# A gated recurrence joined to a PReLU block on one core: level products taken in threes, three tiles folded into one, and a new written-out order

## The chip, the cores and the metric

The kernel runs on one core of a Trainium2 chip. The metric is device time in microseconds (us) for one launch. The engines that matter are TensorE (PE in the profile; its weight loads are PEld), VectorE (DVE), ScalarE (ACT), GpSimd (POOL) and SyncE (SP), which issues every DMA of this kernel.

## What is computed

A complex gated linear recurrence per batch and head, and then two matrix products with a PReLU between them:

```python
# B, H, S, D = 4, 8, 768, 48
a_n = (a_re, a_im) * min(mag, 0.999) / (mag + 1e-6)      # mag = |a|
for t in range(S):
    S_c = a_n[t][:, None] * S_c + outer(k[t], v[t])      # S_c complex, D x D per head
    y[t] = q[t] @ real(S_c)
x = y as (B*S, H*D)                                      # 3072 x 384
h = x @ w_in                                             # 384 x 2048
g = max(h, 0) + alpha * min(h, 0)
out = g @ w_out                                          # 2048 x 384
```

All of it is in fp32, and every product is an fp32 product on PE.

## The kernel before

The sequence is cut into chunks of 128 tokens. One chunk of one batch, with all 8 heads, is a unit; there are 4 x 6 = 24 units, and units 0 to 5 are the chunks of batch 0.

**Gates.** `gates` runs seven times (one, two and three chunks for batch 0, then three chunks each). It turns `a_re` and `a_im` into phases, which are running products of the unit-length gates, and into decays, which are products of the magnitudes over 1, 2, 4, ... tokens. Both go out to DRAM (`phs`, `decs`) and come back for each unit as the tiles `PP` (phases) and `T` (decays, 96 x 8 x 256). Most of the gates' instructions are DVE's (L257 to L425) and ACT's.

**A unit.** `unit` first turns queries and keys, both in the tile `KQ` (96 partitions: real and imaginary parts of 48 dimensions), by their phases: one DVE product over 2048 elements per partition (L648). The tokens of the chunk then interact in six levels, h = 1, 2, 4, 8, 16, 32. In level h, blocks of h tokens are taken in pairs, and the queries of the second block of a pair meet the keys of the first. The loop over levels does four things for each h:

- ACT copies the keys' half of that level into a packed tile `W` (L719, 512 elements; not for h = 1).
- `meet` issues 32 small products on PE into a PSUM tile `lv` (L662); the queries are read as strided halves of `KQ`. Each fp32 product stands in the trace as two matmuls, so a level shows as x32 with 16 products for each of two halves of the heads.
- `step` multiplies `KQ` in place by the decays of that level (L701, DVE, 1024 elements), which also makes it ready for the next level. Since it writes what `meet` reads, it waits for PE.
- `mask_out` moves `lv` to `A{h}` under a mask, on DVE (L686) for h up to 8 and on ACT (L683) for 16 and 32.

After the levels the keys are transposed on PE (L736) and copied by ACT into the tile `KT` (L738). PE multiplies them with `V` into the chunk's contribution to the state (L747), multiplies the `A` tiles with the values `VL` into `Y` (L768), and adds the part of the incoming state (L793). DVE moves the state on (L777, L780). ACT copies `Y` to the tile `yT` (L807), SP writes that to DRAM (`ysc`, L812) and reads it back as `xT` (L825).

**The matrix products.** `features` makes 128 rows of `h` with three matmuls (L841), ACT takes the negative part (L848), DVE adds the scaled rest (L850). `outputs` multiplies by `w_out` (L860), ACT moves the sums out (L870), SP writes them (L873). These products run for one or two units at a time, as soon as their `xT` is there.

**What sets the order.** Each of these parts is a Python generator that yields before each instruction. The string `ORDER` says which generator goes on next, letter by letter (A to G the gates, J to N the loads and weights, O to l the units, n and o the matrix products). It was written by a planner ahead of time; the costs in `yield DVE(...)`, the rings `R[...]` and the names in `done` are that planner's input and do nothing on the chip. Each engine therefore runs a fixed queue, in order, and waits on semaphores that the tile framework sets from the data. A tile that is allocated again waits until its last reader is through: `T` has two buffers, `KQ` three, `V` and `VL` one.

Of the kernel before, what the change touches and what calls it, by code (L numbers as in the profile page):

```python
# [18 lines left out]
P = 128  # L19
# [11 lines left out]
    "AAAAAAAAAABBAMMABMAAAAAMNAAAMMAAAAAAAAABKAAAAAAJKBBNBAKJANAAAJONNAAAAAAOBNOAAAAAAAAAAAJAAAKKAAAAAAKK"  # L31
    "KBABKLMAMKKKAAAAAAAAAAAAABBAAAAAAAAAALLLNLNOBBBBBBBBBBBBBBBOKKLJBBJBCOCNBBBBNNBBBNNNKNBBNNBBBBBOPBBO"
    "BBOOBBBBBBBLLBBBBBPCPPBBBBBBBBBBBOBJBBBBCBBBNBCBBJBPMMJBLBBBLBOPBLMLJJJPPBBCLBOBONOPBBMCCCCCPNPPCLCN"
    "CCCNNCCOPPKJCPCCJMPPJJJJPCNCOCCCCCCCCPOOOOCCCONNNPPQQCOCMCMDPPPPPPPPPPPPPPPPPNPPCNCNCCCNCPONPOCCCQCN"
    "NPKCQCCCPCPCJQQQPQQQCCCCOCCCCQCPNOJQQCOJDJPJJPPKQPDDONJDQCCCCCCCCCQCCOOCQCDQQOLOCCCCCCCDKMRnQQQMKQQK"
    "KKNCKOKOCCCCKMRJQoOCCQQQQNQoJCDQoCCOCLOCCNCCQONLoooLLLDLLDNNDLLDoooDDLoRoNLoRDoRNNDRDRooLLNRJRRDDDDD"
    "NQRoRQKoQQQRDKDJQEREoDONJDDDMDDDQooooDoDooooooRQooooooQooEDoooDoRRRRoooOooOOooooooDRRRJRoJDSooooooRD"
    "RoRRLooQQooELoSOOOLLLLLLLDDDLLLRQQQSRRKKoLDEooSoQooOoDRooRooLoSoDoooEDDooRoooRRROSRRRREoooooQRREDDDD"
    "SDDDDDDoDEESJJSJEEQDJJRJJJSKSSSTSDDLLLRRRRRRLLLESSSDLLTSDEnToTDDSTSETTSSSSLSJTSSSLLDDDDDDDDEEDDDDooS"
    "LLLoKTSooJSoEooSEoDDDDSEETSSSSSSJJSSSSETTTDJEEETDJooEEEEoUTJJJJLLoEooEEJTooDSoooooEoooTDDDTDoSSSSSoL"  # L40
    "LLLLLLooooUTooULLooEooooULJETDTooDooooooDDTDUoooTTooooLooDUoDooKLTTDooooTToooooDDDTETToUUoooTooToTTT"
    "TTnoDoooooooooTLLLUUoooKooLLLLLUTUoLooLooFEJLTUUUULoooooEoJUEooooooUUUUUUEJooEULEEooooooooUoTKEEEToo"
    "EEUVoTToTUUoEoooVVoooooEooooooVUJVVoUFoVUUooTVoUVVUVEUUJJJJUEEEEEEEEEEEEUoUJJTLTVUVFVoVoFWooFVJVVooo"
    "VFooooUUUVVVJUWVKVVUVWWoooooVLLWLLLLLWLLEEEEEEEEEEEEEEEELVVoVLLoWWoLJVVoWoVUoVWVVVooEooooJEEUWWWoVVV"
    "VWVVVVoWWJJJJJJXooEFnFooEEoEELLLLLLLLKJEFLoooVEoooEEooLEooWLLLWXoWLooooWWEoooEooooKEXEWWWKoVVooooooo"
    "KXooEooooXWJWJXXoooWooooWWFoVVoWVXWooooooWWFXFWWWFEWWFFFFGFXooLJLLLLLLXWooooooWFWFXXJFoooFooooFWoFXX"
    "oLLFoGooooJJooooooJFoWFXXXFWFFFWFFFoFooWFoXFFWXooooooFooooooooooXXXXYooooooooGJFWWFXXFXYooFFoooXLLXX"
    "LFFooooooooooLoooYXGLoooXJoooooGYXXFXXFFXXXXXFFFFFFFJYYFJnYJXoGYoooooJFFFFFFFFFFFFFFFLFJJYZFoooooooL"
    "ooGoYZYXXXGJYYZooXooZZoGoooooYooYXoFooooYYYYYYYYYZZoooZFZFFFooooFXJYZoLLLoYoYJYoLLLLLLLKYoYoYooZGLLY"
    "YKYYYYJFYZYYJKXFFFGGooYYJYLLLJLFFLoooooaFFFoYLFFFoFoJJJooZLFZYYYGYYaGLoLLoLLooooooooFLLFoFFFoooooooo"  # L50
    "ooooZoooaZaJZaoooGoZaJZnGZZZZZaooooooooooooaaooaGaZZoooaooZoJoooJGoZZooZoZoooZaHZZZGGoGGGGGGGZZZZZGZ"
    "GaZKKHLGGGoooooaGGoooooooGooobooGoaoooaoaaaaaoooLoGGbooobbZaaaoaaZooaJZZZLJoLLLLLLLLLLoGGGGaaoooGboG"
    "GJoooZaJJoabboooooooaaaaaaaaGHJZHGJJbbbbGGGLGGooooooHoooobaobJJaGGGGGGGGaaaooJJboocooooooobbcoGGbcHb"
    "ooGbLJJKooooooooooooocbGbHcHcLGLcGGKooooooLLbHbLcbbaabGGGGGGooooobbKcGbGJGJGcLLGGGooooHGGcobbbcHoooo"
    "bbLooooLLLLbbbnbcGHbbbbbJGGGdoooooGoLLoocbGGGGGccbooooJJboooGKobGGoGHooLLLLLLoooGHbbbboLooooooooGcLL"
    "LdddccccHdooooocccooooooocdcccdooJoddoLoooooHJcdocLHdJoHdHKHdcoJJooooooocccccIIccoccceooJJooHLLLoooo"
    "oooLoLdeLcHHcccHHHHccccoLLLHHLHHHHnooHoHHHLooooooooHJooooeIdLLLooooooooddooooooeeeHHHHdooHoHHdHeeooo"
    "oooooodddddeooooooodJdoJoeooHHHHHHHHHHHoodoodododeoododooodeedddddddHHdHHHHHHIeeKKeeKHJJooJfooooIooo"
    "ooeeeKeddfoLLdeeooeoeoooJooLooooddLLHHHHHHHHHHHHHHJeedIeeeLfooLLoLLooefLLLLeIofdooeeeHHeeeeeeHHefIIf"
    "IfHfJHHJHJdJooooooeeJJJJJeeeoeegLJHLHHLLofoLLLLLLLofIoooooooooIHooLJffooJoHoooooHogofHoHHIoooooIoooo"  # L60
    "noffoHHooooogfoofoooooffIffffLgoogoooofgooLoffIfJoofoIfIIooJoIfoofooooffffffffffgKggooooohLLLooLhogo"
    "oIoLgghgoooooJJILLLoooLLLffILLfhIIIgghoooooooooohgooJJhgfJJfhhKffggIgggKgooohoooohhggggJghooohoogogo"
    "IgIgooooggIgggggggIhJhoLLgLgIIIIJgIogooooKKoIoooIhooLooILhIoooooooggKJIIIIIIIIJJoooooiLIhoooIIIIoIoo"
    "oooihnooIhhhhihhiooooIiooooLLLLLLiihhLLohohoooooohohohoooohhIIIIhhIhhhhhhJJJIooooooooooJJLiioihiioio"
    "JIoLooLiiijoooooIIIooooIIIioIIIIIIIIIIoiiiiiihhhhhjLLhjLoLLLLLLLiJIIIIIIIoooooojooooojoiijjjoooiooio"
    "jiiooooiLhIIIIIoIoioiiiiiiJLLLLLILooooooLLoooiIioooiiiiiIijjoIiiiIIooooooooooooonJooJJJJooojjjjooooo"
    "ooooooooooooJoLLjjoojojjoojoLkojLjjoooooooooojjkokoooooojjkkjookkoooojjjooLooooLjkjjjjJkkooojjkjjkoo"
    "oooJoooooooookJJokjjJJLllLooLokLkoLoLLLjjkkLkkkLLLLLkkjJjjkooooooooooooJkollkokkJoooooooooookllllooj"
    "kokooJJJlJokoooookkkkJkkkkkkkkkllLLlkLLooomkkkoooolooooooLollooooolloJooomloooonoooooooooooooooooooo"
    "oooooooooollllJlmmooooooooooolmmlooooooolllooolLLLLolomLLLLLllooooooooollloolmlmmmmoooooooomlllloooo"  # L70
    "ooooooooooomlmlmlmoolommllllnoooooooooooooommLmmmoooooooooooooooooooooooooomoLomLooooomommoLLLLLoooL"
    "LLmmmLLooooooooooooooooooooooooooooooooooooooooooommmmmmmmmoommmmmoooooomnoooooooooooooooooooooooooo"
# [30 lines left out]
def kernel(  # L103
# [46 lines left out]
    LEVELS = [1 << i for i in range(6)]  # L150
# [16 lines left out]
    masks, by_row = {}, {}  # L167

    def mask(h):

        m = work.tile([P, P // h, h], F32, tag="W", name="mask", bufs=2)
# [12 lines left out]
    for h in (16, 32):  # L184
        by_row[h] = []
        for m in range(HC // h):
            t = consts.tile([P, 1], F32, tag=f"rows{h}_{m}", name=f"rows{h}_{m}")
            nc.vector.tensor_reduce(out=t, in_=ident.rearrange("p (i m h) -> p m i h", i=2, h=h)[:, m],
                                    axis=mybir.AxisListType.XY, op=ALU.add)
            by_row[h].append(t)  # L190
# [5 lines left out]
    def step(*args, **kwargs):  # L196
# [5 lines left out]
        KQ=3, PP=1, T=2, V=1, W=2, KT=1, St=3, yT=1, xT=2, raw0=1, raw1=1, raw2=1, g0=0, g1=0, g2=0, ot=2, top=2,  # L202
# [7 lines left out]
    bias_tiny = consts.tile([P, 1], F32, tag="bias_tiny")  # L210
    nc.vector.memset(bias_tiny, TINY)
    bias_one = consts.tile([P, 1], F32, tag="bias_one")
# [8 lines left out]
    def gates(g, b, c0, c1):  # L221
# [139 lines left out]
        def three(dst, re_im, k, t):  # L361

            yield ACT(1.5 * k, t)
            nc.scalar.copy(dst[:, 1:3], re_im)
            t = yield ACT(k, t)
            nc.scalar.activation(dst[:, 0], re_im[:, 1], AF.Copy, scale=-1.0)  # L366
            return t
# [585 lines left out]
```

## Time and profile before

| | us |
|---|---|
| median of 3 runs | 863.18 (861.69 to 864.44) |
| the profiled execution, its own time | 859.8 |
| its span on the core | 858.1 |
| PE busy | 704.7 |
| DVE busy | 655.6 |
| ACT busy | 427.1 |
| POOL busy | 186.3 |
| first of the `features` matmuls (L841) starts at | 129.9 |

The span is the time from the first to the last instruction; 1.7 us lie around it. A group's line gives source line, engine, operation, tiles and shapes, the count, the busy time, the mean duration of one, and then the engine's idle time just ahead of these instructions with what ended it. PE's matmuls overlap each other, so a matmul's duration is longer than its distance to the next one: in the rows of the timeline, work is read from start to start.

### The profile page before, as it was taken

What the parts mean: (1) busy time and instruction counts of PE and PEld (TensorE: products, weight loads), DVE (VectorE), ACT (ScalarE), POOL (GpSimd) and SP (SyncE); (2) the same over time, 40 slices, a digit from 0 to 9 for tenths busy, and PEclk for the clock granted to TensorE, in tenths of its full rate; (3) what the DMA queues carried; (4) which work ended last, traced back from release to release, by engine and by line L of the source; (5) the groups of instructions that cost most, each with busy time, mean ns of one, the idle gap of its engine ahead of it and who ended that gap; (6) DMA issues with size and microseconds to landing.
All of it is one profiled execution on the core that took longest, in us unless ns stands there. A gap on an engine that the chain in (4) does not pass through costs nothing.

```text
span 858.1 us, 26855 instructions
## 1 busy us (share of the span) xinstructions
PE 704.7 (82%) x11488; PEld 529.1 (62%) x11488; DVE 655.6 (76%) x996; ACT 427.1 (50%) x913; POOL 186.3 (22%) x293
## 2 busy tenths in 40 slices
PE   0000414976898999999999999999999999999998
PEld 0000313655676777777777777777777777777776
DVE  5999999999976899789978987798867665444212
ACT  7757578576434565554555554654334234233221
POOL 5212323457313200440034005300052000000000
PEclk9999965896999999999999999999999999999999
DMA  7689977977688778669684787865674766221110
GB/s 222 170 211 232 269 175 178 241 154 154 170 194 165 159 195 207 125 135 227 160 182 110 180 216 147 158 170 127 176 155 74 173 121 134 63 51 38 39 39 9
DMA packets 194559, 130.92 MB, mean 153 GB/s; under 512 B 74504, under 2 KB 186248, under 8 KB 194440
## 3 DMA queue, kind: packets, MB, share of 16 engines
q1 hardware_dynamic: 194440, 129.20, 64.9%
q8 instruction: 90, 1.47, 0.8%
q14 instruction: 29, 0.24, 0.1%
HBM read 100.82 MB, written 35.71 MB: 159 GB/s over the span
## 4 chain that ended last, share of the span: by engine, by line
PE 74%; DVE 15%; SPq 3%; issue 3%; DMA 3%; ACT 2%; DVEq 0%; ACTq 0%
PE ps_o L860 29%; PE ps_h L841 29%; PE ps_lv L662 5%; PE ps_y L768 4%; DVE KQ L701 3%; PE ps_kv L747 3%; PE ps_y L793 3%; SPq L556 2%; DVE gate L336 2%; PE ps_kt L736 2%; DMA V<-in_v_dram 1%; DVE gate L338 1%; DVE gate L316 1%; DVE gate L296 1%; DVE gate L422 1%
## 5 line engine op out<-in xcount | busy, mean ns | idle before, releaser
L841 PE MATMUL ps_h<-xT,w_in_sb 128*128 128x256 f32 (+1 forms) x1344 | 303.4, 357 | 0.0
L860 PE MATMUL ps_o<-w_out_sb,g_sb 128*128 128x384 f32 x768 | 297.5, 501 | 7.2 <-DVE g_sb L850 7.1
L841 PEld LDWEIGHTS ps_h<-xT,w_in_sb 128*128 128x128 f32 x1344 | 233.8, 193 | 69.9 <-issue 1.7
L701 DVE TENSOR_TENSOR KQ<-KQ,T 96x1024 f32<-96x1024 f32 x144 | 178.3, 1248 | 44.1 <-PE ps_lv L662 41.1
L848 ACT ACTIVATE g_sb<-ps_h 128x256 f32<-128x256 f32 (+1 forms) x224 | 78.9, 353 | 235.8 <-PE ps_h L841 235.1
L850 DVE SCALAR_TENSOR_TENSOR g_sb<-g_sb,al,ps_h 128x256 f32<-128x256 f32 (+1 forms) x224 | 97.5, 437 | 126.8 <-ACT g_sb L848 126.4
L860 PEld LDWEIGHTS ps_o<-w_out_sb,g_sb 128*128 128x128 f32 x768 | 137.4, 192 | 58.0 <-DVE g_sb L850 9.7
L662 PE MATMUL ps_lv<-KQ,W 96*32 96x32 f32 x3840 | 56.5, 205 | 57.5 <-ACT W L719 54.1
L719 ACT COPY W<-KQ 96x512 f32<-96x512 f32 x120 | 74.3, 623 | 55.4 <-DVE KQ L701 54.1
L662 PEld LDWEIGHTS ps_lv<-KQ,W 96*32 96x32 f32 x3840 | 44.6, 116 | 83.0 <-ACT W L719 62.4
L662 PE MATMUL ps_lv<-KQ 96*32 96x32 f32 x768 | 12.0, 206 | 68.2 <-DVE KQ L648 52.6
L511 POOL TENSOR_SCALAR top<-top 128x768 f32<-128x768 f32 x16 | 43.5, 2721 | 84.3 <-ACT top L503 84.0
L648 DVE TENSOR_TENSOR KQ<-KQ,PP 96x2048 f32<-96x2048 f32 x24 | 55.0, 2292 | 0.0
L662 PEld LDWEIGHTS ps_lv<-KQ 96*32 96x32 f32 x768 | 9.5, 119 | 71.8 <-DVE KQ L648 52.6
L336 DVE TENSOR_TENSOR gate<-gate 128x576 f32<-128x576 f32 (+5 forms) x84 | 48.3, 575 | 3.1 <-ACT gate L308 1.3
L768 PE MATMUL ps_y<-A,VL 64*48 64x64 f32 x2304 | 42.2, 223 | 8.6 <-issue 6.8
L683 ACT ACTIVATE A<-ps_lv,rows 128x64 f32<-128x64 f32 x144 | 39.2, 331 | 19.4 <-PE ps_lv L662 19.0
L336 POOL TENSOR_TENSOR gate<-gate 128x72 f32<-128x72 f32 x42 | 19.0, 451 | 127.2 <-ACT gate L366 124.4
L768 PEld LDWEIGHTS ps_y<-A,VL 64*48 64x48 f32 x2304 | 39.6, 125 | 11.0 <-issue 8.9
L422 DVE TENSOR_TENSOR gate<-gate 128x1152 f32<-128x1152 f32 (+2 forms) x36 | 43.5, 1233 | 0.1
L807 ACT COPY yT<-ps_y 48x256 f32<-48x256 f32 x96 | 32.0, 366 | 21.1 <-PE ps_y L793 20.4
L686 DVE TENSOR_TENSOR A<-ps_lv,mask 128x256 f32<-128x256 f32 x96 | 39.5, 414 | 0.0
(100 smaller groups left out, 774.5 us busy)
## 6 DMA issues: line engine op xcount, KB each, us to landing
T<-decs SPq DMA_DIRECT2D x48, 384.0 KB
PP<-phs SPq DMA_DIRECT2D x48, 193.5 KB
KQ<-in_q_dram SPq DMA_DIRECT2D x48, 192.0 KB
decs<-gate SPq DMA_DIRECT2D x7, 1152.0 KB
phs<-gate SPq DMA_DIRECT2D x14, 576.0 KB
KQ<-in_k_dram SPq DMA_DIRECT2D x40, 192.0 KB
vsc<-in_v_dram SPq DMA_DIRECT2D x48, 144.0 KB
VL<-vsc SPq DMA_DIRECT2D x24, 288.0 KB
```

The lines of the kernel that those rows point to most:

```text
L336: on(4 * k).tensor_tensor(out=m, in0=w[:, 1::-1].unsqueeze(2).to_broadcast([P, 2, 2, k]), in1=pairs_of(u), op=ALU.mult)
L422: TT(out=m[:, a], in0=U5[:, 1 + a], in1=turned(off3, o)[:, a].unsqueeze(1).unsqueeze(3).to_broadcast([P, L // 2, nb, 2]), op=ALU.mult)
L511: nc.gpsimd.tensor_scalar(out=top, in0=top, scalar1=F64_SMALL, scalar2=None, op0=ALU.max)
L648: nc.vector.tensor_tensor(out=KQ, in0=KQ, in1=bass.AP(tensor=PP.tensor, offset=PP.offset, ap=[PP.ap[0], (1, 2), (P + 1, H), (1, P)]), op=A ...
L662: nc.tensor.matmul(t[64 * i + j:64 * i + j + HC // 2, p], lhsT=weights(4 * i + p)[:, j:j + HC // 2], rhs=q_[:, m * g:m * (g + 1)], start=T ...
L701: nc.vector.tensor_tensor(out=x, in0=x, in1=m, op=ALU.mult)
L719: nc.scalar.copy(W.rearrange("p n t -> p (n t)").rearrange("p (m h) -> p m h", h=h), halves(KQ[:, 1].rearrange("p n t -> p (n t)"), h)[:, ...
L768: nc.tensor.matmul(o, lhsT=Vp[h][64 * i:64 * i + 64, s, e_ * D:(e_ + 1) * D], rhs=a, start=False, stop=False)
L841: nc.tensor.matmul(p, lhsT=w_in_sb[:, f // 2, kk, f % 2 * P:(f % 2 + 1) * P], rhs=x_of[m][:, kk], start=(kk == 0), stop=(kk == NK - 1))
L848: nc.scalar.activation(gt, p, AF.Relu, scale=-1.0)
L850: nc.vector.scalar_tensor_tensor(out=gt, in0=gt, scalar=al_1[:, f:f + 1], in1=p, op0=ALU.mult, op1=ALU.add)
L860: nc.tensor.matmul(sums[0], lhsT=gt[:, c * P:(c + 1) * P], rhs=w_out_sb[:, f], start=(f == 0), stop=(f == NF - 1))
```

## The change

- Levels are taken in two visits, (1, 2, 4) and (8, 16, 32). Within a visit the products of the three levels are issued one after the other on PE, into three parts of one `lv` tile; they wait until the last level's operands are there.
- For the first two levels of a visit, keys and queries come from a copy: for h = 1 it is written by the turn itself, whose one product over 2048 elements becomes two over 1024 (one into the copy `WQ`, one in place); for h = 2, 8 and 16 ACT copies both halves (1024 elements instead of 512). For h = 4 ACT copies the keys alone as before, for h = 32 nothing is copied. So `step` no longer waits for PE in four levels of six, but for ACT's copy in three of these.
- The three `mask_out` of a visit follow the last product.
- `KT` and `yT` are gone. The transposed keys go to the first 128 columns of the decays' tile `T` (in two ACT copies per half instead of one, since the padding is now filled from PSUM), and the outputs go to the same columns later. `T` is therefore free only when the unit's outputs have left for DRAM, and no longer after the state's update.
- Small constant tiles are put into one; `run`, `runs` and `begin` of the gates have one buffer instead of two; `mask` uses a `WQ` buffer.
- `ORDER` is written anew as a whole.

The numbers of products, DMAs and gate instructions stay as they were: PE has 2304 level products in the program before and after, SP 755 DMAs.

```diff
 ORDER = (
-    "AAAAAAAAAABBAMMABMAAAAAMNAAAMMAAAAAAAAABKAAAAAAJKBBNBAKJANAAAJONNAAAAAAOBNOAAAAAAAAAAAJAAAKKAAAAAAKK"
...
+    "AAAAAAAAAAAAAAAAAAMMMMBAANBJAAAAANMMNJJAAAAAAAAAAAONAAAANAAAOOAANAAAAAAAAAAAAAJANOAOBNAAAAMMKNLNAAAL"
...
-    LEVELS = [1 << i for i in range(6)]
+    VISITS = [(1, 2, 4), (8, 16, 32)]
+    LEVELS = [h for visit in VISITS for h in visit]
...
-                    L["T"] = T = work.tile([D2, H, TL], F32, tag="T", name="T", bufs=2)
+                    L["T"] = T = work.tile([P, H, TL], F32, tag="T", name="T", bufs=2)
...
-        nc.vector.tensor_tensor(out=KQ, in0=KQ, in1=bass.AP(
-            tensor=PP.tensor, offset=PP.offset, ap=[PP.ap[0], (1, 2), (P + 1, H), (1, P)]), op=ALU.mult)
...
+        WQ = work.tile([D2, 2, H, HC], F32, tag=f"WQ{first_slot}", name="WQ", bufs=1)
+        nc.vector.tensor_tensor(out=WQ, in0=some(1, -1), in1=phases(1, 0), op=ALU.mult)
+        r = yield DVE(H * P)
+        nc.vector.tensor_tensor(out=some(0, 1), in0=some(0, 1), in1=phases(0, 2), op=ALU.mult)
...
-            t = ps.tile([P, HP, HC // 2], F32, tag="lv", name="ps_lv", bufs=2)
+            if not shared:
+                shared.append(ps.tile([P, 3, HP, HC // 2], F32, tag="lv", name="ps_lv", bufs=2))
+            t = shared[0][:, at]
...
-        for h in LEVELS:
-            w = k_
-            if h == 1:
-                weights = lambda n: KQ[:, 1, n].rearrange("p (m s) -> p m s", s=2)[:, :, 0]
-            else:
-                w = yield ACT(H * HC, k_, takes=(R["W"],))
-                W = work.tile([D2, H, HC], F32, tag="W", name="W", bufs=2)
...
-            e, t = yield from meet(h, weights, w, k_)
...
-            step(h)
-            yield from mask_out(h, t, e)
+        for visit in VISITS:
+            ready = []
+            for h in visit:
...
+                elif h != visit[-1]:
+                    held = "WQ"
+                    w = yield ACT(2 * H * HC, k_, takes=(R[held],))
+                    slot = spare.pop(0)
+                    z = work.tile([D2, 2, H, HC], F32, tag=f"WQ{slot}", name="WQ", bufs=1)
+                    nc.scalar.copy(z.rearrange("p i n t -> p i (n t)").rearrange("p i (m h) -> p m i h", h=h), bass.AP(
+                        tensor=KQ.tensor, offset=KQ.offset + h, ap=[KQ.ap[0], (2 * h, H * HC // h), (H * P - h, 2), (1, h)]))
...
+                ready.append((h, keys, queries, held, slot, w))
+                if h != visit[-1]:
+                    k_ = yield DVE(2 * H * HC, w, *[("decays", u)] * (h == 1))
+                    T = L["T"]
+                    step(h, WQ if h == 1 else None)
+            tiles, shared = [], []
+            for at, (h, keys, queries, held, slot, w) in enumerate(ready):
+                e = yield from meet(h, shared, at, keys, queries, w, k_, takes=() if at else (R["lv"],))
...
+            if visit[-1] != 1:
+                k_ = yield DVE(2 * H * HC, e)
+                step(visit[-1])
+            for h, ta, e in tiles:
+                e = yield from mask_out(h, ta, e)
+            R["lv"].put(e)
...
-            nc.scalar.copy(KT[:, 4 * i * D2:4 * (i + 1) * D2].rearrange("p (n d) -> p n d", n=HP), t)
+            nc.scalar.copy(T[:, 4 * i:4 * (i + 1), 0:D2], t)
+            nc.scalar.copy(T[:, 4 * i:4 * (i + 1), D2:P], t[:, :, 0:P - D2])
...
-                    yT = work.tile([P, 2, 2, P], F32, tag="yT", name="yT", bufs=1)
+                    yT = T[:, 0:4, 0:P].rearrange("p (i s) t -> p i s t", i=2)
                 nc.scalar.copy(yT[64 * e_:64 * e_ + D, i], Y[64 * e_:64 * e_ + D, i])
...
-                              yT[64 * e_:64 * e_ + D].rearrange("p i s t -> p (i s) t"))
-        R["yT"].put(t)
+                              T[64 * e_:64 * e_ + D, 0:4, 0:P])
+        R["T"].put(t)
```

## The prediction

> **What bounds the kernel now.** I read the page's busy slices first, then busy time by stretch, to see which engine limits which stage.
>
> ```profile
> PE   0000414976898999999999999999999999999998
> ...
> DVE  5999999999976899789978987798867665444212
> ```
>
> ```profile
> 0.00:225.00 225.00, 82.42 (x1964) 64.56 (x1965) 208.45 (x373) 151.99 (x255) 87.65 (x96) 0.86 0.82 202
> 225.00:280.00 55.00, 49.47 (x904) 37.80 (x903) 42.66 (x61) 23.10 (x59) 10.10 (x27) 0.94 0.76 165
> 280.00:858.00 578.00, 572.84 (x8625) 426.78 (x8623) 404.53 (x564) 252.03 (x600) 88.51 (x170) 1.00 0.59 132
> ```
>
> The columns are the stretch, its length, and busy us of PE, PEld, DVE, ACT, POOL, then the granted clock. There are two stages with a handover. Up to 225 us DVE is busy 208 of 225 us: it makes the gates and the first units, and PE has little to do. From 280 us on PE is busy 573 of 578, and DVE has 173 us of slack. So a microsecond counts where it is DVE's before about 225 us, and where it is PE's after about 280 us; ACT (152 of 225, then 252 of 578) and POOL bound neither.
>
> Third, the timeline of PE in the PE-bound stage, to price the change of kind of product (start, length, line, count):
>
> ```profile
> 575.31 1.45 PE L860 MATMUL ps_o<-w_out_sb,g_sb 128*128 128x384 f32 x4
> 576.70 0.76 PE L662 MATMUL ps_lv<-KQ,W 96*32 96x32 f32 x64
> 577.39 1.56 PE L841 MATMUL ps_h<-xT,w_in_sb 128*128 128x256 f32 x6
> ...
> 588.02 1.45 PE L860 MATMUL ps_o<-w_out_sb,g_sb 128*128 128x384 f32 x4
> 589.41 0.46 PE L662 MATMUL ps_lv<-KQ,W 96*32 96x32 f32 x32
> 589.79 1.56 PE L841 MATMUL ps_h<-xT,w_in_sb 128*128 128x256 f32 x6
> 591.19 1.45 PE L860 MATMUL ps_o<-w_out_sb,g_sb 128*128 128x384 f32 x4
> 592.48 1.46 PE L841 MATMUL ps_h<-xT,w_in_sb 128*128 128x256 f32 x6
> ```
>
> From start to start: four L860 before another big product take 1.29 us (591.19 to 592.48), before level products 1.39 (588.02 to 589.41). So going in costs 0.10. One level (x32) takes 0.38, two in a row (x64, 576.70 to 577.39) 0.69. Alone a level costs 0.48, as two 0.79: joining a level to another saves 0.17 us of PE.
>
> Last, the groups that the change prices, and who DVE waits for between 195 and 290 us:
>
> ```profile
> L701 DVE TENSOR_TENSOR KQ<-KQ,T 96x1024 f32<-96x1024 f32 x144 | 178.3, 1248 | 44.1 <-PE ps_lv L662 41.1
> L719 ACT COPY W<-KQ 96x512 f32<-96x512 f32 x120 | 74.3, 623 | 55.4 <-DVE KQ L701 54.1
> L648 DVE TENSOR_TENSOR KQ<-KQ,PP 96x2048 f32<-96x2048 f32 x24 | 55.0, 2292 | 0.0
> ```
>
> ```profile
> DVE g_sb L850 <- ACT g_sb L848: 7.3, 4, 3.7
> DVE KQ L701 <- PE ps_lv L662: 5.8, 3, 4.0
> ```
>
> L701 waits 41 us for PE in all, which looks like the thing to remove. But only 5.8 of it (plus 0.8 before) lies up to 290 us; the rest is in the stage where DVE has slack, and is worth nothing.
>
> [...]
>
> **The change part by part.**
>
> *PE visits.* In the program's order, level products stand in 98 separate places before, and in 50 after. From the 32nd output product on (248 us in the trace) it is 80 against 39. 41 x 0.17 = 7.0 us of PE less, nearly all on the path. The seven fewer visits ahead of that point are worth nothing while PE waits for DVE. All mode changes together go from 262 to 173, 210 to 134 in that later part; 76 x 0.10 gives 7.6, the same within the price's error. Packed instead of strided operands: h = 1 reads strided keys and costs 0.28 beside another level, the packed ones 0.31; I take nothing.
>
> *The turn, L648.* 24 x 0.15 = 3.6 us of DVE more; eight turns lie before the handover, so 1.2 on the path; at most 3.6.
>
> *ACT copies.* Three copies of 1024 elements replace four of 512 per unit. From 623 ns (512) and the gates' copies, 1259 (1152), a copy of 1024 should take 1.1 us: 3 x 1.1 + 0.62 against 5 x 0.62 is 0.8 more. The key copies in two parts (384 and 128 from PSUM; 479 ns now, a small one about 0.28) add 0.5. 1.4 us per unit, 11 us up to the handover, onto 152 of 225: hidden by ACT's idle third. If that cover is gone, `step` for h = 4, 16 and 32, which stands behind these copies, holds DVE's queue, and all 11 count.
>
> *Steps without PE.* The 5.8 us of L701's waits may go; but two steps of six still wait for PE, now behind three products (0.31 x 3), and three wait for ACT. I book it in the next item and not by itself.
>
> *Order and handover.* To compare the two orders I sum along the queues. DVE's work in order, each instruction at its mean duration less 0.049 us (the durations add up to 704, busy is 655.6, over 996 instructions: they overlap by that). PE's work in order from its start-to-start distances after 320 us (L841 0.219 and 0.112, L860 0.326, L736 0.083, L662 0.0088, L747 0.0153, L768 0.0145, L793 0.029, and 0.105 per mode change): 683 us before, 674 after. For each PE instruction that waits for DVE, DVE's work up to there plus PE's work from there on is a floor of the span. Before, it is 828.1 at DVE 231 with 597 left for PE, and still 825 at DVE 271. The trace reaches DVE 231 at 253.7 us: 22 us of lag, 11.5 of it in the first 50 us. Trace time plus PE work left gives 846 at 235 us, 857 at 283 us and 852 to 857 from there on. So PE loses its last 11 us between 235 and 283. After, the highest floor of the early part is 824.8 (DVE 233, PE 592), 3.3 lower: the 7 to 9 us of PE, less about 5 by which more of DVE's work, units' and turns' work, stands ahead. Then it falls to 812 by DVE 277, where before it fell by 3: PE has some 10 us of work in stock right after the handover. Of the 11 us of PE idleness there I take 4 as saved, between 0 and 11. The lag of 22 I keep; 6.5 us of lost DVE time from 50 to 225 can hardly get better (say 3), and can get worse by far more.
>
> *T kept until the outputs leave.* No instruction more, but the loads of `T` for unit u+2 now follow the output DMAs of unit u on SP. After the last state update: PE 1 us, four L807 of 0.37 on ACT, a DMA of outputs and one of `T`. The landings that the chain of waits shows are 5.1 to 5.5 us each, so some 13.5 us, during which later DMAs stand behind on SP. In the new order 13 to 26 us of DVE work stand between the state update of u and step 1 of u+2. Zero if all goes in 13 us, which I take; see the slow rival.
>
> *The gates' single buffers and the constants.* `runs` is reused one gate group later, 60 us on at the least: nothing.
>
> *Sum.* -3.3 - 4 = -7.3, span 850.8; with the 1.7 us around it 852.5, against 859.8 for the profiled execution of before. That one lay 3.4 below the median of the runs, so the median should be about **856**.
>
> **The rivals.**
> 1. *Everything in the handover goes.* All 11 us: -3.3 - 11 = -14.3, median 849. For it: the floor falls fast. Against: waits for values and for ACT lie in there too (L850 behind L848, 7.3), and these stay.
> 2. *DVE takes it.* The PE visits are worth their 7 us only if DVE delivers as early; if the lag grows by 4 to 7 (the ACT copies show in the steps, the turns count in full), -0 to -3: median 860 to 863. No change that can be told.
> 3. *Slower: T comes late.* In the DVE-bound stage units follow each other by 21 to 43 us (turns at 50, 93, 126, 170, 191, 213). SP's queue now waits for ACT's output copies up to 9.0 us (L812 behind L807), and that wait is put ahead of the next `T`. If output and `T` need 20 to 25 us rather than 13.5, step 1 of units 4, 5, 6 and 8, with 16 to 25 us of cover, stands still at the head of DVE's queue by about 5 each: +20 - 7 = +13, median about 871. It decides from some 17 us of round trip on. For it: DMA is 0.82 busy up to 225 us. Against: the order was laid out with the loads after the outputs, and step 1 of those units stands later.
>
> The change does what it says in the built program (38 of its visits hold 48 products), so that is no rival.
>
> **How the numbers follow.** A measurement of this kernel can tell about 0.3%, 2.6 us, from no change. Forecast 0.48 (852 to 860); rival 1 0.16; rival 2 0.13; rival 3 0.23. Faster 0.64, the same 0.13, slower 0.23. The range goes from 847 (rival 1 with 2 us more) to 869, most of the way to rival 3; half of that rival and a little below are left out.
>
> **What would show it.** Right: L662 in about 50 visits; a level inside a visit 0.31 us; PE gapless from about 280 us on; DVE's wait for `lv` up to 290 us under 3 us; the turns 1.22 each; ACT's copies near 1.1. Rival 3: step 1 (the first product with `T`) waiting for a DMA of `T`, and SP waiting long at the output DMAs before 250 us. Wrong altogether: PE reaching gapless work later than 290 us, or level products slower than 0.31 us each in a visit of three.

## The result, and the profile after

The changed kernel takes 863.9 us (median of 12, 860.0 to 866.9) against 862.05 for the kernel before (12 runs): ratio 1.0021, 95% interval 1.0005 to 1.0036. A second measurement of the same kernel gave 1.0050 (1.0031 to 1.0069). Forecast was 856 us, 0.7% faster; it is 0.2 to 0.5% slower. The profiled execution took 861.62 us, span 859.9 (before: 859.8, span 858.1).

The slices of PE, and busy time by stretch (stretch, length, busy us of PE, PEld, DVE, ACT, POOL, granted clock):

```profile
PE   0001414667699999999998999999989999999998
```

```profile
0.00:225.00 225.00, 76.78 (x2022) 61.72 (x2023) 205.17 (x368) 156.38 (x251) 85.31 (x93) 0.87 0.80 199
225.00:280.00 55.00, 53.92 (x856) 42.67 (x856) 46.29 (x75) 26.60 (x71) 17.63 (x30) 0.97 0.71 171
280.00:860.00 580.00, 565.29 (x8613) 424.07 (x8611) 405.77 (x579) 269.23 (x616) 105.43 (x170) 1.00 0.58 132
```

PE is busy 53.9 of 55 us in the handover (before 49.5), and its work from 280 us on fell from 572.8 to 565.3, which is 7.5. But it now stands idle there: 14.7 of 580 us, where it was 5.2 of 578. A visit in the timeline of PE (start, length):

```profile
625.42 1.03 PE L893 MATMUL ps_h<-xT,w_in_sb 128*128 128x256 f32 x4
626.38 0.76 PE L682 MATMUL ps_lv<-WQ 96*32 96x32 f32 x64
626.99 0.46 PE L682 MATMUL ps_lv<-KQ 96*32 96x32 f32 x32
627.38 0.70 PE L893 MATMUL ps_h<-xT,w_in_sb 128*128 128x256 f32 x2
```

Three levels take 1.00 us from start to start (626.38 to 627.38), the last part of it the way out. The groups that the change priced, and then waits over the whole run (us in total, times, longest). The last line is the kernel before: there the masks of levels 16 and 32 (L683, now L703) waited for PE:

```profile
L721 DVE TENSOR_TENSOR KQ<-KQ,T 96x1024 f32<-96x1024 f32 x120 | 148.8, 1241 | 44.4 <-PE ps_lv L682 23.8
L744 ACT COPY WQ<-KQ 96x1024 f32<-96x1024 f32 x72 | 78.2, 1086 | 62.7 <-DVE KQ L721 49.9
```

```profile
ACT A L703 <- DVE A L706: 45.2, 19, 4.2
DVE KQ L721 <- DMA T<-decs: 4.4, 4, 1.9
...
ACT A L683 <- PE ps_lv L662: 19.0, 17, 2.5
```

PE's own waits from 280 us on, the two longest in sum after the change and then the longest before it:

```profile
PE ps_y L821 <- issue: 3.5, 1, 3.5
PE ps_kt L789 <- ACT T L792: 3.0, 3, 2.1
...
PE ps_y L768 <- issue: 0.8, 1, 0.8
```

To see when the gain was lost, I add to each moment PE's work that is left at that moment, priced from start-to-start distances, and subtract the same sum of the kernel before. Below zero the changed kernel is ahead:

| at us | 280 | 460 | 500 | 600 | 650 | 840 |
|---|---|---|---|---|---|---|
| after | -9.6 | -9.1 | -5.1 | -3.4 | +0.9 | +2.1 |
| after, second execution | -8.0 | -6.2 | -2.1 | -0.1 | +4.7 | +5.3 |

So the forecast gain (7.3) was there until 460 us, and was given back in single places. Adding up every distance between two products of PE that is over 0.12 us too long, from 280 us on: 2.4 us before, 14.5 after, 15.9 in the second execution. The difference of 12 pays for the gain and the 2 us above it. (`gates` runs nine times, not seven as the description of the kernel has it.)

### The profile page after: what moved, and what is told of

The parts are those of the page before. It is cut to its first block, busy times and chain, and to the rows that moved or that the text cites. A ratio compares the mean times of both kernels' runs of the same rounds, so it can differ in the third digit from the quotient of the medians.

```text
span 859.9 us, 26885 instructions
## 1 busy us (share of the span) xinstructions
PE 696.0 (81%) x11488; PEld 528.5 (61%) x11488; DVE 657.2 (76%) x1020; ACT 452.2 (53%) x937; POOL 208.4 (24%) x293
## 4 chain that ended last, share of the span: by engine, by line
PE 61%; DVE 20%; DMA 9%; issue 4%; ACT 4%; SPq 3%; DVEq 0%; ACTq 0%
PE ps_h L893 24%; PE ps_o L912 24%; DVE KQ L721 4%; PE ps_lv L682 4%; DMA T<-decs 3%; DVE gate L339 3%; PE ps_y L821 3%; PE ps_kv L801 2%; PE ps_y L845 2%; DVE gate L341 2%; DMA VL<-in_v_dram 2%; PE ps_kt L789 2%; DVE gate L427 1%; ACT A L703 1%; SPq L630 1%
## 5 line engine op out<-in xcount | busy, mean ns | idle before, releaser
L721 DVE TENSOR_TENSOR KQ<-KQ,T 96x1024 f32<-96x1024 f32 x120 | 148.8, 1241 | 44.4 <-PE ps_lv L682 23.8
L682 PE MATMUL ps_lv<-WQ 96*32 96x32 f32 x3072 | 40.0, 203 | 99.6 <-DVE WQ L665 61.4
L744 ACT COPY WQ<-KQ 96x1024 f32<-96x1024 f32 x72 | 78.2, 1086 | 62.7 <-DVE KQ L721 49.9
L682 PEld LDWEIGHTS ps_lv<-WQ 96*32 96x32 f32 x3072 | 33.5, 114 | 112.7 <-DVE WQ L665 52.8
L703 ACT ACTIVATE A<-ps_lv,columns 128x64 f32<-128x64 f32 x144 | 36.5, 339 | 48.9 <-DVE A L706 45.2
L516 POOL TENSOR_SCALAR top<-top 128x768 f32<-128x768 f32 x16 | 38.7, 2427 | 80.6 <-ACT top L508 75.4
L859 ACT COPY T<-ps_y 48x256 f32<-48x256 f32 x96 | 31.3, 366 | 28.5 <-PE ps_y L845 27.2
L789 PE MATMUL ps_kt<-ident,KQ 96*128 96x96 f32 x192 | 26.8, 266 | 17.2 <-ACT T L792 10.5
L789 PEld LDWEIGHTS ps_kt<-ident,KQ 96*128 96x128 f32 x192 | 21.9, 151 | 27.7 <-ACT T L792 14.7
L319 POOL TENSOR_TENSOR gate<-gate 128x72 f32<-128x72 f32 (+2 forms) x18 | 25.1, 1395 | 54.2 <-DVE gate L319 53.3
L706 DVE TENSOR_TENSOR A<-ps_lv,mask 128x256 f32<-128x256 f32 x96 | 36.5, 412 | 0.0
```

The source lines that it names most:

```text
L682: nc.tensor.matmul(t[64 * i + j:64 * i + j + HC // 2, p], lhsT=keys(n, g), rhs=queries(n, g), start=True, stop=True)
L703: nc.scalar.activation(a[:, :, cols], t[:, :, at:at + name], AF.Copy, scale=s)
L721: nc.vector.tensor_tensor(out=x, in0=x if x0 is None else x0, in1=m, op=ALU.mult)
L744: nc.scalar.copy(z.rearrange("p i n t -> p i (n t)").rearrange("p i (m h) -> p m i h", h=h), bass.AP(tensor=KQ.tensor, offset=KQ.offset + ...
L789: nc.tensor.transpose(t[:, p], KQ[:, 1, 4 * i + p], ident[:D2, :D2])
```

## The experiments

Theories: **V**, the visits lie on the path (rival **W**, they don't). Then for the 12 us. **A**: all three levels share one `lv` tile, so ACT's masks of 16 and 32 (L703) wait for DVE's mask of 8 (L706), which stands behind a step. **B**: `T`, held until the outputs leave, comes late. **C**: what PE waits for are chains through ACT, DVE and DMA that also start from PE. **F**, formed later: PE waits for its own instructions.

### One: are the visits on the path?

The main lines of the edit (the tile gets a fourth part for the added product):

```diff
             t = shared[0][:, at]
+            if at:
+                nc.tensor.matmul(shared[0][:, 3, 0, 0:1], lhsT=ident.bitcast(BF16)[:, 0:P],
+                                 rhs=ident.bitcast(BF16)[:, 0:1], start=True, stop=True)
```

> The changed kernel, with one tiny full-size bf16 product (one column, into an unused part of the same PSUM tile) put on PE between the first and second and between the second and third level of each visit: 96 interruptions of level products more (its weight load and column are extra work, the output stays as it was). It puts back, twice over, the changes of kind that the visits saved. Theory V (PE's visits lie on the path in the PE-bound stage, as predicted): some 78 of the 96 stand after the handover; at 0.17 us each, and a little for the product itself, the time rises by 13 to 18 us over the changed kernel, PE's busy time from 280 us on rises by as much, and the stalls of PE there stay near 13 us. Rival W (PE has idle time there that swallows it, the saving of 7 us was never on the path): the time rises by under 5 us, and PE's stalls shrink instead.

Measured: 884.1 us, ratio 1.0250 (1.0217 to 1.0284), 17 to 20 us over the changed kernel, where 13 to 18 were expected. In the trace an undisturbed visit of three levels takes 1.38 us instead of 0.96, 0.21 for each interruption, the tiny product included. 68 of the 96 lie after 280 us, which makes 14.4 us. The stalls there did not shrink, they grew, to 20.2 us (14.5 and 15.9 in the changed kernel); most of the rest is this growth. V holds and W falls: PE's visits are paid in full. And the stalls are not PE having run ahead of its feeders. (The 192 added instructions also move the blocks of part four, so the total alone is not the price of the interruptions.)

### Two: the mask, and the hold on T

The edit of the mask (e2), and the main line of the edit of `T` (e3), which also moves 44 loads in `ORDER`. e4 has both:

```diff
-            if visit[-1] != 1:
-                k_ = yield DVE(2 * H * HC, e)
-                step(visit[-1])
+            if visit[-1] == HC // 2:
+                h, ta, e8 = tiles.pop(0)
+                yield from mask_out(h, ta, e8)
+            k_ = yield DVE(2 * H * HC, e)
+            step(visit[-1])
```

```diff
-                    yT = T[:, 0:4, 0:P].rearrange("p (i s) t -> p i s t", i=2)
+                    yT = work.tile([P, 2, 2, P], F32, tag="W", name="yT", bufs=1)
```

> The changed kernel with one exchange on DVE: in the second visit the mask of level 8 goes ahead of the step of level 32, not behind it. Theory A (the three levels share one lv tile, and ACT's masks of 16 and 32 wait for DVE's mask of 8, which stands behind 1.22 us of step; so ACT comes late to the key copies, and PE to the second transposition): ACT's wait for A falls from 45 us to under 15, PE's stalls at the transpositions (464.8, 659 and 691 us; 3.2 us in all) go, and the time falls by 2 to 4 us. Rival B (the late loads of T and what they push on the DMA queues cost the time): ACT waits less, but the time stays within 1 us of the changed kernel, since the stalls near 495 to 506 and at 641 stay.

> The changed kernel with the outputs copied to the tile W instead of T's first columns (W is free then; same size), and the loads of T for a unit put on SP right behind the state update of the unit two before, as in the kernel before, instead of behind its output DMAs (44 places moved, by 1 to 135 steps of the order, 36 in the middle). Nothing else moves. Theory B (T held until the outputs leave makes T late, and makes T, the next KQ and VL share the DMA engines after the same event): DVE's wait for T (4.4 us) goes, VL of the unit at 641 us lands some us earlier, PE's stalls at 482 to 506 and at 641 us (1.1 and 5 us with the slower clock behind) shrink, and the time falls by 4 to 7 us, to about 858. Rival A (ACT's masks): the time stays within 1 us of the changed kernel. If both fail (the order itself makes the stalls), PE's stalls keep their sum of about 13 us and only move.

> The changed kernel with both edits: level 8's mask ahead of step 32, and outputs in W with T loaded right behind the state update. If A and B are each part of it and add up: 6 to 10 us faster than the changed kernel, 854 to 858, which is what was predicted for the change (856). If only one of them is at work, the time of that one's own run. If neither, the time of the changed kernel within 1 us.

Measured: e2 860.7 us, ratio 0.9982 (0.9960 to 1.0005); e3 870.8, 1.0114 (1.0090 to 1.0138); e4 868.5, 1.0086 (1.0061 to 1.0111). With A's edit ACT's wait fell to 19.3 us, where under 15 was expected:

```profile
ACT A L703 <- DVE A L706: 19.3, 16, 3.0
```

and the time fell by 0.4 to 0.7% in e2, and by 0.3% from e3 to e4, where the intervals overlap. So the edit is worth something, but the way from ACT's wait to PE is not the one that A gave. PE's waits at the transpositions were 3.0 us in all, and in e2 2.4 us of them stayed, near 465 us: there DVE's step itself is what the transposition waits for. (The traced execution of e2 was the slowest of its 14, 867.0 us.)

B got no support, and the test has a flaw. DVE's wait for `T` did fall from 4.4 to 0.5 us, without any gain, but the outputs in `W` brought a new wait, for another unit's level 4 to have read `W`:

```profile
ACT yT L859 <- PE ps_lv L682: 20.7, 11, 4.0
```

At 280 us e3 is 7.7 us behind the changed kernel already, and 8 us at 840: after 280 us it loses as much. So the lateness of `T` by itself is not what cost the time; what the hold costs otherwise, this run cannot tell.

### Three: the same kernel again, and two ways to cover the stalls

e5 is the changed kernel. e6 moves ten loads in the order of SP (the moves in `ORDER` are given in words here and below):

```diff
 V of unit 18
+VL of unit 18 (10 loads)
 KQ of unit 19, ysc of unit 17, PP of unit 19, xT
-VL of unit 18 (10 loads, in between and behind)
```

e7 brings matrix products ahead on PE, as for the outputs of unit 18 here; e8 adds the edit of e2:

```diff
 outputs L821 of unit 18, first pair
+L893, L912: 4.6 us of features and outputs
 outputs L821 of unit 18, second pair
-L893, L912: 4.6 us of features and outputs
```

> The changed kernel once more, with nothing edited. It shows which of PE's stalls after 280 us belong to the kernel and which to one execution. If the order places the waits, the same places stand still again: the second transposition of unit 12 (2.1 us near 465), the outputs of unit 18 for VL (3.6 us near 641), and the sum of stalls after 280 us is again 11 to 15 us. If they are accidents of one execution, under half of these places stand still again.

> The changed kernel with ten loads of one unit (the VL parts of unit 18) moved ahead on SP, right behind its V, so that they no longer stand behind the loads of KQ, PP, an xT and the outputs of unit 17. Nothing else is moved. Theory S (PE's stalls are made one by one by where the order puts loads and products, and each is worth its length): VL lands before the outputs of unit 18 are due, the stall of 3.6 us near 641 and the slow products behind it (1.4 us) go, and the time falls by 3 to 5 us. Rival D (the burst of transfers that start together, 1.4 MB in some 15 us, makes the last one late, whichever it is, as in the run with T loaded early): another transfer of the burst (xT or T) comes late in its place, and the time stays within 1.5 us.

> The changed kernel with matrix products (features and outputs, with their ACT and DVE steps) brought ahead in the order at six places where PE stood still in the traced execution: before the level 4 of unit 8 (1.7 us of products), the second transposition of unit 12 (3.2), its second state product (2.0), the outputs of unit 18 for its second pair (4.6), and the second transposition of units 19 and 20 (1.7 and 1.5). Each engine has the same work. Theory S: the five stalls (8.6 us, and 1.4 of slow products behind one) are covered by the products put ahead, and the time falls by 5 to 9 us, to 855 to 859. Rival C (the unit's chain over ACT, DVE and DMA is what PE waits for; putting the products ahead delays the chain's own start by as much, since it also runs through PE, ACT and DVE): the stalls return a little later in the same units or the next, their sum stays above 11 us, and the time stays within 2 us of the changed kernel.

> The same six places with products brought ahead, and level 8's mask ahead of step 32 on DVE, which alone gave 860.7 against 863.9. If the two add up and theory S holds: 852 to 856, faster than the kernel before by 0.7 to 1.1%. If rival C holds: within 1.5 us of 860.7.

Measured: e5 864.9 us, 1.0050; e6 862.15, 1.0033 (1.0016 to 1.0050); e7 872.6, 1.0146 (1.0126 to 1.0167); e8 872.1, 1.0137 (1.0118 to 1.0156).

The order places the stalls: in e5 the second transposition of unit 12 waits 2.06 us again, and unit 18's outputs stand still again. In e7 the stalls grew to 22.9 us: PE then waited at other places of the same units (1.89 and 3.36 us for `VL`, 3.08 for the state). The mask added nothing that could be told there (e8). So the idea of covering the stalls falls. That the products put ahead delayed the unit's own chain fits C, but C's numbers missed as well: it had the time within 2 us of the changed kernel, and it rose by 8 to 9.

e6 gave the hint. `VL` was loaded earlier, yet PE stood still at the same products (3.36 us), and no other transfer of data took its place. The time lies 1.5 us below e5 by the ratios, 2.7 by the medians, between what D allowed and what S expected; the mechanism is neither's. Here is the place in the changed kernel and then in e5, from the timeline of PE (in brackets the idle time ahead):

```profile
636.26 1.10 PE L821 MATMUL ps_y<-A,VL 64*48 64x64 f32 x62
640.88 0.81 PE L821 MATMUL ps_y<-A,VL 64*48 64x64 f32 x34 [3.52 <-issue]
641.62 2.93 PE L893 MATMUL ps_h<-xT,w_in_sb 128*128 128x256 f32 x6
```

```profile
644.45 0.87 PE L821 MATMUL ps_y<-A,VL 64*48 64x64 f32 x34 [3.71 <-issue]
```

The stall lies in the middle of a row of outputs. The products behind it use the same `A` and `VL` tiles as some in front of it, and in the built program the first of them has no wait on any semaphore; "issue" says that the profile has no releaser either. So no data can be late. I numbered PE's instructions (23,588; an fp32 product is four, two weight loads and two matmuls). The stalls without a wait stand at the same numbers in kernels with different orders: 722, 2019, 12434 and 17906 in the changed kernel; 722, 2019 and 17906, to within one, in each of e2, e3, e5 and e6. The page's list of DMA queues has a row that I had passed over:

```profile
q8 instruction: 90, 1.47, 0.7%
```

90 packets of 16,384 bytes over PE's instructions: a block for every 262. The first of them starts at 72.2 us, 19 us after PE's first product (52.85). That these packets bring PE's instructions is my reading of the row and of its name, and no more than that so far; part four puts it to the test.

### Four: moving the blocks against the work

Tiny bf16 products at the head of PE's stream, in its idle first microseconds (1.2 to 3.9 us), move every block boundary against the work (the kernel before takes `ident` for `nothing`):

```diff
+    pad = ps.tile([P, HP, D2], F32, tag="misc", name="ps_pad")
+    for _ in range(32):          # 64 and 96 for 128 and 192 instructions
+        nc.tensor.matmul(pad[0:D2 // 2, 0, 0:1], lhsT=nothing[:, 0:D2 // 2],
+                         rhs=nothing[:, 0:1], start=True, stop=True)
```

> The changed kernel with 64 more instructions at the head of PE's stream: 32 tiny bf16 products of one column into an unused PSUM tile, in the first 50 us, when PE has nothing to do. All else is as it was. Theory F (half of PE's new stalls are late fetches of its instructions, which come as blocks of 16,384 bytes through the DMA engines: stalls without any wait on a semaphore, at the same numbers in PE's stream in kernels of different order, 722, 2019, 7491, 12434, 17906): the block boundaries move by 64 instructions against the work, so the stalls without a wait move to other work, some vanish and some appear; the stall of 3.7 us in the outputs of unit 18 goes or changes by over 1 us, and the median differs from 863.9 (864.9) by 1 to 5 us in one of the three runs with padding at least. Rival G (these stalls come from data, on the DMA queues or another engine, which the profile does not name): the same stalls stand at the same products, and the median stays within 1 us in all three.

> The same with 128 instructions (64 tiny products) at the head of PE's stream, half a block. Theory F: stalls without a wait lie at other products than in the changed kernel and than with 64; the stall in the outputs of unit 18 is gone or smaller by over 1 us. Rival G: as the changed kernel within 1 us, with the stalls at the same products.

> The same with 192 instructions (96 tiny products). Theory F: again other places; medians of the three and of the changed kernel spread over 2 to 6 us. Rival G: within 1 us.

> The kernel before with 128 instructions at the head of PE's stream (64 tiny products from a constant, in idle time). If the kernel before had its block boundaries by luck where they do no harm (one stall without a wait after 280 us, 0.98 us), theory F gives 1 to 4 us more than before. If its single levels, which never put more than 64 records of small products in a row outside the outputs, leave room for the fetches wherever the boundaries lie, or rival G holds, the time stays within 1 us of before.

> The kernel before with 64 instructions at the head of PE's stream. Known so far: 128 give 894.7 for the kernel before, and 877.0, 891.1 and 873.9 (64, 128, 192) for the changed one. From both traces, [...] I estimate 9 to 17 us more for this one. If the changed kernel's visits of three made PE's stream the more sensitive one (rival), the kernel before rises by under 5 us here.

> The kernel before with 192 instructions at the head of PE's stream. The same estimate gives 13 to 20 us more than the kernel before, so 875 to 883; under 5 us more if its single levels are the less sensitive stream. Mean over the four paddings: if both kernels suffer alike, the two means lie within 3 us of each other (that of the changed kernel is 876.6); if the change's own gain of 7 us is there and only hidden by the place of the blocks, the mean of the kernel before is 880 to 885.

Measured (the last two with the runs of part five; stalls are those over 0.85 us without a wait, from 280 us on):

| instructions added | before: us, ratio | stalls | after: us, ratio | stalls |
|---|---|---|---|---|
| 0 | 862.05, 1 | 1, 1.0 us | 863.9, 1.0021; 864.9, 1.0050 | 3, 5.9 us; 4, 7.6 us |
| 64 | 884.8, 1.0266 (1.0239 to 1.0294) | 10, 17.1 us | 877.0, 1.0167 (1.0133 to 1.0202) | 7, 16.2 us |
| 128 | 894.7, 1.0370 (1.0340 to 1.0399) | 12, 22.2 us | 891.1, 1.0327 (1.0294 to 1.0360) | 11, 27.1 us |
| 192 | 887.4, 1.0278 (1.0242 to 1.0313) | 9, 15.7 us | 873.9, 1.0137 (1.0097 to 1.0177) | 5, 13.6 us |

F holds, and it is far larger than I expected (1 to 5 us at first; 9 to 17 and 13 to 20 for the last two, which cost 23 and 25): instructions that take up to 4 us of idle PE cost 9 to 33 us. The stall in the outputs of unit 18 is gone with 128. With 64 it stands about 32 matmuls earlier in the work (2.9 us), with 192 it stands 32 later (3.1 us), which is where the moved boundaries lie. The worst case in the waits and at one place, with 128 added to the changed kernel (L824 are the outputs there):

```profile
PE ps_y L824 <- issue: 26.0, 11, 4.4
```

```profile
594.28 1.06 PE L824 MATMUL ps_y<-A,VL 64*48 64x64 f32 x60
599.69 1.30 PE L824 MATMUL ps_y<-A,VL 64*48 64x64 f32 x36 [4.35 <-issue]
```

The traces show the blocks in two more ways. Counted in PE's matmuls, neighbouring stalls of this kind lie whole multiples of 126.7 apart, to within 4, in every trace of the table that has more than one, of both kernels and all paddings; with 128 added to the changed kernel, the distances 381, 1395, 1394 and 1015 are 3, 11, 11 and 8 times that. 126.7 is also what PE issues in the mean from the start of one q8 packet to the next in the changed kernel's trace (11,277 matmuls over 89 distances); with as many weight loads that makes 253 instructions, near the 262 from the program's count. And the packet itself is there: in each of the nine stalls of that trace that left PE idle for over 0.85 us after 280 us, a packet of q8 landed 1.2 to 1.6 us before PE went on (1.46 and 1.60 us before, in the two such stalls of the changed kernel).

Why small products make it likely: a visit puts 192 instructions into 1.0 us, state products and outputs of a unit put 328 into 2.8 us, where a matrix product of 0.65 us has four. By these rates, as an estimate, 253 instructions last 1.3 us in a visit, 2.2 in such outputs and some 41 in matrix products, while a packet of q8 took 0.9 to 1.7 us from its start to its landing in the changed kernel's trace. When a packet is asked for, no trace shows. And it is the number that counts, not the work: with 64 and with 128 instructions added PE stands still at number 12434 again, though products with the state (L845) stood there in the changed kernel, and a features product and outputs stand there now.

Both kernels sit at a place of the blocks that suits them, as far as these four places tell. The mean ratio over the four is 1.0229 before and 1.0167 after (with 1.0036 for zero added): the changed kernel is 0.6%, some 5 us, faster in this mean. But at the single places it lies between 0.4% slower and 1.4% faster, and four are too few to call the mean shown. My rival that visits of three starve PE more than single levels found no support: in these places the kernel before suffers as much or more.

### Five: why the block near 641 us is late

In the changed kernel `T` of unit 19 and `KQ` of unit 20 are loaded together at 628 to 632 us, behind the outputs of unit 17, and the DMA engines are full until 641 us (busy share 1.12 from 630 to 637.2 us and 1.15 from there to 640.8). `KQ` is not wanted before 660. e13 moves it behind the outputs of unit 18, in the trace from 628.9 to 648.2 us:

```diff
 T of unit 19
-KQ of unit 20 (4 loads), PP of unit 20 (first)
...
+KQ of unit 20 (4 loads), PP of unit 20 (first)
```

e14 is e13 with the mask of e2.

> The changed kernel with five loads moved later on SP: the four of KQ and the first of PP for unit 20 stand behind the outputs of unit 18, some 8 us later; KQ is wanted by the turn at 660 us, 30 us after it was loaded, so nothing waits for it. Theory F2 (a block of PE's instructions comes late when it has to pass bulk transfers in the DMA engines: in the changed kernel T, KQ, VL and an xT, 2.2 MB, start together behind the outputs of a unit, and the block fetched at 638 us stood behind them): the stall of 3.7 us inside the outputs of unit 18 falls by 1.5 us or more and with it the slow products behind, and the median falls by 2 to 5 us against the changed kernel (863.9; 864.9). If the block's place in the stream is all that counts and the load of the DMA engines does not: within 1 us.

> The same with level 8's mask ahead of step 32 (860.7 alone, about 1 us below the kernel before). If both add up: 856 to 859, faster than the kernel before by 0.3 to 0.7%. If the late load does nothing: 860 to 861.5.

Measured: e13 861.6 us, ratio 0.9998 (0.9982 to 1.0013); e14 855.5 us, ratio 0.9927 (0.9906 to 0.9948). Against the changed kernel's ratios (1.0021 and 1.0050) that is 0.2 to 0.5% less for e13, as expected, and 0.9 to 1.2% less for e14, a little more than expected. The packet shows why: in the changed kernel the block wanted behind the stall starts to move at 638.22 us and lands at 639.28, when PE has stood still since 637.36. In e13 its packet starts at 637.10, some 130 matmuls before it is wanted, lands at 638.35, and PE runs on without a stall. The outputs of unit 18 in e14 run through (L823 there), and what remains is the wait of unit 12's transposition for DVE:

```profile
633.74 1.15 PE L803 MATMUL ps_kv<-V,T 64*64 64x48 f32 x64
634.71 0.29 PE L814 MATMUL ps_y<-ident,nothing 64*48 64x256 bf16 x4
634.82 1.81 PE L823 MATMUL ps_y<-A,VL 64*48 64x64 f32 x96
636.56 1.56 PE L895 MATMUL ps_h<-xT,w_in_sb 128*128 128x256 f32 x6
```

```profile
462.55 0.55 PE L791 MATMUL ps_kt<-ident,KQ 96*128 96x96 f32 x4 [2.63 <-DVE KQ L721]
```

```profile
280.00:854.00 574.00, 564.73 (x8618) 424.64 (x8616) 407.09 (x580) 270.88 (x618) 106.32 (x170) 1.00 0.58 134
```

PE is idle for 9.3 us from 280 on instead of 14.7 (stalls 8.5 instead of 14.5 to 15.9). Two edits that move a mask by one place and five loads by 14 to 19 us bring the time to what was forecast, 855.5 against 856, below both kernels. That the numbers meet is in part chance: the forecast had PE gapless from about 280 us on, and in e14 it is not.

## Why the prediction was wrong, step by step

- *PE visits.* Right. Predicted 7.0 us less on PE; measured 7.5 from 280 us on, in 50 visits as counted. (A mode change, as the prediction calls it, is a change of shape from one product to the next, such as 128\*128 to 96\*32; that all shapes pay the 0.10 us read at the level products was an estimate.) A level added to a visit costs 0.29 us (I took 0.31), and e1's interruptions cost 0.21 each (I took 0.17).
- *The turn.* 1236 and 1243 ns for the two halves against 2292: 0.19 each where I took 0.15, so 4.5 us of DVE for 24 units and 1.5 on the path. Small, and by typical durations (1215 and 1222 against 2280) it is 0.16. The 0.15 was my estimate; the profile before gives 0.14 (a typical step over 1024 elements, L701, took 1217 ns, the turn 2292).
- *ACT copies.* 1086 ns (I took 1.1 us) and 291 ns for the small key copy (0.28). ACT is busy 25 us more, and that was not wholly hidden: up to 280 us DVE waited 4.7 us for these copies, none before. It ate most of the 5.7 us by which DVE's waits for `lv` fell there. (The steps behind the copies are those of levels 2, 8 and 16, not 4, 16 and 32 as the prediction has it.)
- *Order and handover.* Right up to 280 us: 8.0 to 9.6 us ahead, predicted 7.3 in all. DVE's wait for `lv` up to 290 us is 0.9 us (predicted under 3). (DVE's idle time from 50 to 225 us before was 5.0 us by the stretches, not 6.5; nothing hangs on it.)
- **The step that failed** is what this one left out, and what "What would show it" put as "PE gapless from about 280 us on". I took one kind of floor, DVE's work before a PE instruction, saw it fall to 812, and concluded that PE would have 10 us in stock and no more waits. PE was 8.0 to 9.6 us ahead at 280 us, and then stood still for 12 us more than before, in waits that are not in that floor. The largest part, 4.9 to 6.6 us in the two executions, is PE's own instructions: 5.9 to 7.6 us after 280 us, 1.0 before. Nothing in my sums had a place for it; parts four and five show this cause. The other part that an edit moved is ACT's queue: with three levels in one tile, masks on ACT wait for a mask on DVE (45.2 us; none before). The prediction listed the shared tile in the change and did not ask what two readers of it do to each other. Before, with a tile for each level, these masks waited for PE (19.0 us). What makes one reader of the tile wait for the other is not shown: a tile for each level of a visit was not tried. Moving the mask is worth 0.4 to 0.7% by itself and 0.7% on top of e13, and nothing that could be told in e8. How it reaches PE is not shown: PE's waits for ACT at the transpositions are 3.0 us, and the edit left most of that as a wait for DVE.
- *T kept until the outputs leave: zero.* Not settled. The direct price is small (DVE waits 4.4 us for `T`, none before), and rival 3's 13 us in the DVE-bound stage did not come. But it puts `T` behind the outputs, next to the following `KQ`, and e13 shows that transfers bunched there make an instruction block late (its packet starts at 638.22 us with them and at 637.10 without). How much of the bunching is the hold's and how much the new order's stays open.
- *Rivals.* Rival 2 came nearest, 860 to 863 and no change that can be told, but for the wrong reason: DVE was not late, PE was ahead at 280 us. Its number is luck.

Left open: the rest of the stalls (8.5 us in e14, 2.4 before), of which 2.7 are unit 12's transposition, and which place of the blocks is best; only four were tried.

## What to carry to other kernels

Once an engine is nearly gapless, count what it waits for besides data: here its own instructions came over the DMA engines (the 90 packets of q8), and rows of small products used them up faster than they came (stalls of 3.52 us in the changed kernel and 4.35 with 128 instructions added). A stall "issue" in the middle of a row with no new operand was the sign; moving the stream by half a block with idle instructions showed what was at stake (27 us and more with 128), and until that is done, a difference of 1% between two orders of such a kernel says little about the change in them. When tiles are joined, list the engines that read each: a join on PE's side chained two other engines together here (ACT waited 45.2 us for DVE).

## What the runs showed of the hardware that I had not expected

The size of the instruction stalls (above). And what a stall costs behind it: after 3.5 us of idleness PE's granted clock was low for most of the next 3.6 us, from the stretches of the changed kernel:

```profile
630.00:637.20 7.20, 7.20 (x156) 5.53 (x155) 4.83 (x7) 3.68 (x13) 2.15 (x3) 1.00 1.12 201
637.20:640.80 3.60, 0.17 (x11) 0.01 (x1) 3.27 (x5) 1.48 (x3) 0.00 (x0) 1.00 1.15 239
640.80:644.40 3.60, 3.52 (x41) 2.84 (x41) 0.00 (x0) 0.00 (x0) 0.00 (x0) 0.58 0.19 23
```

The clock is 1.00, 1.00 and then 0.58: three features products take 2.93 us instead of 1.46, so the stall of 3.7 us costs about 5. (e13, without the stall, takes 5.4 us less for the same 60 matmuls.) After 2.4 and 2.6 us of idleness (unit 12's transposition in e2 and e14) the next 3.6 and 4.0 us had 0.57 and 0.59 as well. The length does not decide alone: one and the same wait of 2.06 us, at unit 12's transposition, was followed by 3.41 us at half clock in e6 and e13 and by none in the changed kernel, and e6's stall of 3.36 us by none. I have no rule for it from these traces.
